# Second norms turned by transposing DMAs, gate and up weights in three pieces, and the last later-token output product inside the first feed-forward block

## Chip, core and metric

The kernel runs on one core of a Trainium2 chip. The metric is the device time of one execution in microseconds. The core has TensorE (PE, with its weight loads listed apart as PEld), VectorE (DVE), ScalarE (ACT), GpSimd (POOL) and SyncE (SP). Each runs its own list of instructions in order and waits on semaphores; DMAs are issued from SP and ACT and move data between device memory and the on-chip buffer.

## The reference

A block of a recurrent transformer over 2048 tokens of width 640, followed by a gated feed-forward layer. `x` is normed, cut into 64 segments of 32 tokens, and each segment is put behind 8 memory rows; attention runs over these 40 rows with 32 heads of 128, and the first 8 rows of the result are the memory of the next segment.

```python
for s in range(n_seg):
    xs = x[:, s * seg_len:(s + 1) * seg_len, :].copy()
    h = jnp.concatenate([mem, xs], axis=1)
    q = jnp.einsum('btd,dhe->bhte', h, Wq)
    k = jnp.einsum('btd,dhe->bhte', h, Wk)
    v = jnp.einsum('btd,dhe->bhte', h, Wv)
    scores = jnp.einsum('bhqe,bhke->bhqk', q, k) * scale
    scores = jnp.where(mask[None, None], scores, -1000000000.0)
    p = _softmax(scores, axis=-1)
    o = jnp.einsum('bhqk,bhke->bhqe', p, v)
    o = jnp.einsum('bhte,hed->btd', o, Wo)
    mem = o[:, :M, :].copy()
    outs.append(o[:, M:, :])
...
gate = jnp.einsum('bsd,df->bsf', x, W_gate)
up = jnp.einsum('bsd,df->bsf', x, W_up)
gate = gate * (gate > 0)
h = gate * up
return jnp.einsum('bsf,fd->bsd', h, W_down)
...
h = x + _A_ref(_layernorm(x, axis=-1), A_mem0, A_Wq, A_Wk, A_Wv, A_Wo, A_seg_len)
h2 = h + _B_ref(_layernorm(h, axis=-1), B_W_gate, B_W_up, B_W_down)
```

F, the width of the feed-forward layer, is 1728. Types are bf16, with sums in 32 bits.

## The kernel before

The work has three stages. First the weights Wq, Wk, Wv and Wo are loaded, and the projections of the first part of the rows that do not depend on the recurrence are made. Then the 64 segments run one after the other (`segment`, L1813). Last, the feed-forward layer runs in 4 blocks of 512 tokens (`ffn`, L1687).

A segment's own tile of 32 rows (`xT`) holds the 8 memory rows and its first 24 tokens. The last 8 tokens ("later tokens") do not depend on the recurrence before attention and are handled apart: `ln1r(r)` (L1486) norms the later tokens of 16 segments at a time (r = 0 to 3), turns them on TensorE with 20 transposes (L1496), and evicts them to `xr`; `rest` (L1538) makes their projections, which go through the staging tiles `stg` to the scratch tensors `scr_qk` and `scr_v`, and `load_rs` (L1592) brings them back for each segment. Nine of the sixteen groups of `rest` are made ahead of the segments; the others are filler between the segments' own products. The output product of the later tokens, `rest_o` (L1608, products at L1617), is made for 8 segments at a time; it is filler too, except for the last 8 segments (z = 7), whose product follows the last segment in one piece of 128 matmuls (L2018). `rest_out` (L1628) stores it into `scr_o`.

The second norm, `ln2(k)` (L1650), runs for each of the 16 tiles of 128 tokens: load x and the attention's output, add, store the sum to `scr_h`, norm, turn on TensorE with 20 transposes (`tr2`, L1669, products at L1673), evict. For k below 4 the eviction writes `xn2T`, the moving operand of the first feed-forward block; for the others it writes a tile that is stored, turned, to `scr_n` and loaded again by `ffn` (L1692). Tiles 14 and 15, which need the last segments, are called `tn2`; the others run as filler during the segments.

`ffn(b)` works on 14 chunks of the width F, 13 of 128 and one of 64 for gate and up together. For each chunk, 5 matmuls make the gate and 5 the up product (`proj`, L1695, products at L1699), ACT applies the relu, DVE multiplies (L1718). Then for 4 tiles of 128 tokens, 14 pairs of matmuls (512 and 128 columns; the second uses the weights that the first has loaded, L1732 and L1510) make the down product, DVE adds `h` in two instructions (L1739), and SP stores the tile (L1742).

The feed-forward weights lie where Wq, Wk and Wv lay. `load_f` (L2032) loads gate and up in two pieces each, 896 and 768 columns; the first waits until Wq's place is free (key `B0`), the second also for the eviction of the last segment's output (key `("osb", 1)`); Wd and the rest follow.

No order is written out by hand. `op` records each operation with the keys it reads (`r=`), writes (`w=`) and the buffers it takes (`x=`), with an estimated duration; `_Sched.schedule` then puts the operations in a fixed order on each engine, by a level that is the length of the work behind an operation plus a number from the table `BIAS` for its name and segment. `ENGINE` says which of ACT and DVE makes an eviction. The result is a static list for each engine; at run time there are only semaphore waits.

## Time and profile before

| | us |
|---|---|
| median of 3 runs | 1036.55 |
| lowest and highest | 1035.58, 1037.53 |
| the profiled execution's own time | 1038.79 |
| span of the profiled execution | 1037.1 |

The mean granted TensorE clock was 0.998. In the second part of the page, the busy tenths of the engines are given in 40 slices of the span, so that one slice is 25.9 us; slices 1 to 3 are the weight load and the early projections, slices 4 to 33 the segments, and slice 33 on the feed-forward layer:

```profile
PE   6999999999999999999999999999999989999998
DVE  5865676677767666876676577667766734232242
ACT  2236555456556664665465555645654633121210
DMA  9995111122112221311121122112221155110111
```

A digit 9 means 90% or more. The DMA engines are full while weights are loaded: in the first three slices, and to half in slices 33 and 34.

### The profile page before, as it was taken

The page shows a single profiled execution, that of the slowest core. Times are in us where ns is not written, and L with a number is a line of the kernel's source. Part 1 is how long each engine was busy: PE and PEld are TensorE (multiplying, and loading weights), DVE is VectorE, ACT ScalarE, POOL GpSimd, SP SyncE. Part 2 cuts the span into 40 slices and gives each one's busy share as a digit, 9 for nine tenths or more (in the row PEclk, how much of TensorE's full clock was granted, in tenths as well). Part 3 has the DMA queues.
Part 4 walks back from the last instruction along what each step waited for, and adds up shares of the span by engine and source line. Part 5 has one row for each costly group of instructions (what it writes and reads, how often), then busy time and mean ns, then how long its engine had stood idle before and what let it go on. Part 6 is the DMA issues. An engine that isn't in the chain of part 4 may idle for free.

```text
span 1037.1 us, 53187 instructions
## 1 busy us (share of the span) xinstructions
PE 991.5 (96%) x24820; PEld 531.0 (51%) x23828; DVE 643.2 (62%) x1400; ACT 492.0 (47%) x1165; POOL 107.7 (10%) x262
## 2 busy tenths in 40 slices
PE   6999999999999999999999999999999989999998
PEld 2345545555555555655555555555555554344443
DVE  5865676677767666876676577667766734232242
ACT  2236555456556664665465555645654633121210
POOL 2241101001000100111011001000100010000000
PEclk9999999999999999999999999999999999999999
DMA  9995111122112221311121122112221155110111
GB/s 327 405 314 128 40 38 44 34 63 65 50 27 73 55 59 33 93 46 37 50 81 54 29 66 76 44 33 74 65 52 39 59 178 175 60 58 20 32 33 44
DMA packets 119212, 84.26 MB, mean 81 GB/s; under 512 B 71556, under 2 KB 115148, under 8 KB 118988
## 3 DMA queue, kind: packets, MB, share of 16 engines
q1 hardware_dynamic: 113900, 76.56, 24.5%
q8 instruction: 191, 3.13, 1.3%
q10 hardware_dynamic: 5088, 4.30, 1.2%
q14 instruction: 33, 0.27, 0.1%
HBM read 55.05 MB, written 25.69 MB: 78 GB/s over the span
## 4 chain that ended last, share of the span: by engine, by line
PE 89%; DVE 4%; DMA 4%; issue 1%; POOL 0%; ACT 0%; SPq 0%; ACTq 0%; POOLq 0%; DVEq 0%
PE ps L1532 46%; PE ps L1699 11%; PE ps L1906 7%; PE ps L1925 7%; PE ps L1732 5%; PE ps L1617 3%; PE ps L1873 3%; PE ps L1510 2%; DMA scr_qk<-stg 2%; PE ps L1848 2%; PE ps L1834 1%; DVE xT L1646 1%; DMA big<-in_A_x_dram 1%; DVE xm L1643 1%; DMA Wq<-in_A_Wq_dram 1%
## 5 line engine op out<-in xcount | busy, mean ns | idle before, releaser
L1372 ACT ACTIVATE tok<-ps 128x512 bf16<-128x512 f32 x230 | 136.6, 597 | 158.5 <-PE ps L1532 152.5
L1532 PE MATMUL ps<-Wk,xT 128*32 128x512 bf16 x2560 | 183.3, 379 | 4.2 <-DVE xT L1646 3.1
L1532 PE MATMUL ps<-Wq,xT 128*32 128x512 bf16 x2560 | 169.7, 380 | 12.6 <-DVE xT L1646 11.8
L1532 PE MATMUL ps<-Wv,xT 128*32 128x512 bf16 x2560 | 178.3, 379 | 0.0
L1955 DVE STREAM_TRANSPOSE QT<-tok 128x512 bf16<-128x512 bf16 x128 | 90.9, 711 | 40.1 <-ACT tok L1372 37.5
L1955 DVE STREAM_TRANSPOSE KT<-tok 128x512 bf16<-128x512 bf16 x128 | 90.7, 708 | 34.2 <-ACT tok L1372 32.5
L1373 DVE CAST oT<-ps 128x320 bf16<-128x320 f32 x130 | 63.6, 491 | 76.6 <-PE ps L1878 73.5
L1532 PEld LDWEIGHTS ps<-Wq,xT 128*32 128x32 bf16 x2560 | 65.7, 97 | 85.5 <-DVE xT L1646 25.4
L1532 PEld LDWEIGHTS ps<-Wk,xT 128*32 128x32 bf16 x2560 | 63.8, 96 | 62.2 <-DVE xT L1646 9.3
L1906 PE MATMUL ps<-Wo,oT 128*32 128x320 bf16 x2048 | 92.0, 301 | 1.5 <-DVE oT L1373 1.1
L1925 PE MATMUL ps<-Wo,oT 128*32 128x160 bf16 x4096 | 86.2, 233 | 6.3 <-issue 3.8
L1716 ACT ACTIVATE g<-ps 128x512 bf16<-128x512 f32 (+1 forms) x56 | 33.4, 596 | 121.7 <-PE ps L1699 121.7
L1372 ACT ACTIVATE oT<-ps 128x320 bf16<-128x320 f32 x126 | 55.0, 437 | 67.9 <-PE ps L1878 65.4
L1925 PEld LDWEIGHTS ps<-Wo,oT 128*32 128x32 bf16 x4096 | 74.7, 97 | 21.5 <-DVE oT L1373 11.7
L1843 ACT ACTIVATE E<-ps 128x224 bf16<-128x224 f32 x128 | 45.7, 357 | 82.9 <-PE ps L1838 82.9
L1718 DVE TENSOR_TENSOR gT<-g,ps 128x512 bf16<-128x512 bf16 (+1 forms) x56 | 37.9, 686 | 68.0 <-PE ps L1699 57.3
L1532 PEld LDWEIGHTS ps<-Wv,xT 128*32 128x32 bf16 x2560 | 60.7, 96 | 36.8 <-DVE tok L1373 0.3
L1820 POOL COPY QT<-RS 128x256 bf16<-128x256 bf16 x64 | 25.6, 400 | 476.8 <-PE ps L1838 476.7
L1373 DVE CAST tok<-ps 128x512 bf16<-128x512 f32 x90 | 59.5, 662 | 22.1 <-PE ps L1532 22.0
L1372 ACT ACTIVATE ps<-seed 128x384 f32<-128x384 bf16 x110 | 50.6, 487 | 36.5 <-DVE half L1914 34.9
L1699 PE MATMUL ps<-xn2T,Wg 128*128 128x512 bf16 x260 | 63.3, 380 | 0.0
L1699 PE MATMUL ps<-xn2T,Wu 128*128 128x512 bf16 x260 | 63.2, 380 | 0.0
(95 smaller groups left out, 1451.2 us busy)
## 6 DMA issues: line engine op xcount, KB each, us to landing
RS<-scr_qk SPq DMA_DIRECT2D x63, 128.0 KB, 2.3
big<-in_A_x_dram SPq DMA_DIRECT2D x36, 160.0 KB, 3.0
Wq<-in_A_Wq_dram SPq DMA_DIRECT2D x10, 512.0 KB, 6.9
Wk<-in_A_Wk_dram SPq DMA_DIRECT2D x10, 512.0 KB, 7.8
Wv<-in_A_Wv_dram SPq DMA_DIRECT2D x10, 512.0 KB, 7.8
Wo<-in_A_Wo_dram SPq DMA_DIRECT2D x8, 640.0 KB, 11.3
scr_qk<-stg ACTq DMA_DIRECT2D x32, 128.0 KB, 6.0
scr_v<-stg SPq DMA_DIRECT2D x32, 128.0 KB, 2.9
```

The lines of the kernel that those rows point to most:

```text
L1372: return e.activation(dst, src, ACTF.Copy)
L1373: return e.tensor_copy(dst, src)
L1532: o = pe.matmul(out, lhs[c], rhs, start=(c == 0), stop=(c == DC - 1), skip_group_check=True)
L1617: o = pe.matmul(bank(bk)[p0:p0 + 32, 0:2 * SLICE], oTr[b][:, h, 32 * y:32 * y + 32], cols(h, 2 * a, 2 * a + 2), start=(h == 0), stop=(h == ...
L1699: o = pe.matmul(bank(bk)[:, 0:TB], lhs(c), xT[:, :, c * 128:(c + 1) * 128], start=(c == 0), stop=(c == DC - 1))
L1716: op("act", lambda a, t=t, lo=lo, hi=hi, bg=bg: a.activation(g1[t.at][lo:128, :], bank(bg)[0:hi, 0:TB], ACTF.Relu), r=["B2"], x=[bg, t], d ...
L1718: op("dve", lambda v, t=t, lo=lo, j=j, bu=bu: v.tensor_tensor(gT[lo:128, j, :], g1[t.at][lo:128, :], bank(bu)[lo:128, 0:TB], ALU.mult), r= ...
L1732: pe.matmul(bank(ba)[:, 0:512], lhs, Wd[:, j, 0:512], start=(j == 0), stop=(j == FC - 1), skip_group_check=True)
L1843: op("act", lambda a: a.activation(E[:, g, :, 0:56], sco(BS[g]), ACTF.Exp, scale=SCALE), r=["table"], w=[("E", g)], x=[BS[g]], dur=0.36, n ...
L1906: o = pe.matmul(bank(BA)[p0:p0 + 32, 0:2 * SLICE], oT[:, 4 * jj + i, XR:40], cols(h, 2 * b2, 2 * b2 + 2), start=(i == 0 and jj < 2), stop= ...
L1925: o = pe.matmul(bank(BW)[32 * j:32 * j + 32, 0:SLICE], oT[:, 16 + 4 * jj + i, XR:40], cols(h, j, j + 1), start=(i == 0 and jj == 0), stop= ...
L1955: op("dve", lambda v, tb=tb, dst=dst: v.transpose(dst, tok[tb.at][:, :].rearrange("p (h r) -> p h r", r=32)), w=[("QT" if p == 0 else "KT" ...
```

## The change

Five things are edited, and the tables `BIAS` and `ENGINE` are replaced by others, so that the order of operations differs everywhere.

1. Turns by DMA. `ln2` has no TensorE transposes and no eviction after them. For k below 4, SP issues a transposing DMA from the normed tile to `xn2T`. For the others the normed tile is stored as it is, and `ffn` loads it with a transposing DMA. `ln1r` does the same for r = 2 and 3; r = 0 and 1 stay on TensorE.
2. Gate and up weights come in three pieces, of 384, 640 and 640 columns. The first waits for `B0`, the others also for the last segment's output eviction. The loads of the normed tiles of block 1 (and 3) wait for that eviction as well.
3. The last later-token output product (z = 7) stands in the first feed-forward block: it waits for the up products of chunks 0 to 2 (keys `guz`), and chunk 3's gate product waits for it (key `roz`).
4. The norms 14 and 15 are recorded after the first block's chunks.
5. The last token tile's down product is made in two passes, 14 matmuls of 512 columns and then 14 of 128 with their own weight loads; each half is added and stored by itself.

The estimate of one POOL copy rises from 0.8 to 1.08 in the early stage; that alters the planner's order only.

```diff
+FPIECES = ((0, 384), (384, 1024), (1024, 1664))
...
+        slot = r == 1 and EARLY > 4
+        if r > 1:
+            op("sp", lambda e: e.dma_start_transpose(xr[slot][:, :, :], big[xt.at][:, :]), x=[xt], w=[("xr", slot)],
+               dur=0.5, lat=3.5, chan=("tp", 2), name="ln1rT", xfer=0.5)
+            return
...
-        bt = B("tr")
-
-        def tr2(pe):
-            o = None
-            for c in range(DC):
-                for a in range(4):
-                    o = pe.matmul(bank_bf(bt)[32 * a:32 * a + 32, c * 128:(c + 1) * 128],
-                                  big[at.at][:, c * 128 + 32 * a:c * 128 + 32 * a + 32], ident[:, :], is_transpose=True)
-            return o
-
-        op("pe", tr2, r=["ident"], x=[at, bt], dur=0.28, n=40, name=nm + "T")
         if k < 4:
-            either(lambda e, en: copy(e, en, xn2T[0][:, u, :], bank_bf(bt)[:, 0:640]),
-                   r=["late"], w=[("xn2T", 0, u)], x=[bt], dur=ev(640, True), name=nm + "Tev")
+            op("sp", lambda e: e.dma_start_transpose(xn2T[0][:, u, :].rearrange("p (c t) -> p c t", c=DC), big[at.at][:, :]),
+               r=["late"], w=[("xn2T", 0, u)], x=[at], dur=0.5, lat=3.5, chan=("tp", 2), name=nm + "T", xfer=0.5)
             return
-        either(lambda e, en: copy(e, en, big[x2.at][:, :], bank_bf(bt)[:, 0:640]), x=[bt, x2], dur=ev(640, True),
-               name=nm + "Tev")
-        op("sp", lambda e: e.dma_start(scr_n[k], big[x2.at][:, :]), w=[("scr_n", k)], x=[x2], dur=0.4, lat=2.2,
+        op("sp", lambda e: e.dma_start(scr_n[k], big[at.at][:, :]), w=[("scr_n", k)], x=[at], dur=0.4, lat=2.2,
            chan=("n", 2), name=nm + "nd")
...
         for u in range(4 if b else 0):
-            op("sp", lambda e, u=u: e.dma_start(xT[:, u, :], scr_n[4 * b + u]), r=[("scr_n", 4 * b + u)] + (["B1"] if home else []),
-               w=[("xn2T", home, u)], dur=0.4, lat=2.4, chan=("xn", 4), name="xnld")
+            op("sp", lambda e, u=u: e.dma_start_transpose(xT[:, u, :].rearrange("p (c t) -> p c t", c=DC), scr_n[4 * b + u]),
+               r=[("scr_n", 4 * b + u)] + (["B1", ("osb", 1)] if home else []), w=[("xn2T", home, u)], dur=0.5, lat=3.5, chan=("tp", 2), name="xnld")
...
         for j in range(FC):
             t = _Slot("g1", range(3))
+            if b == 0 and j == 3:
+                z = NSEG // 8 - 1
+                rest_o(z, B("rest"), (0, 8), [("guz", n) for n in range(3)], "roz")
+                rest_out(z)
             if j < FC - 1:
                 bg, bu = banks(0, 1, 2, 3), banks(0, 1, 2, 3)
-                proj(bg, lambda c, j=j: Wg[:, c, j * 128:j * 128 + 128], ("Wg", 2 * j // FC), (), [bu])
-                proj(bu, lambda c, j=j: Wu[:, c, j * 128:j * 128 + 128], ("Wu", 2 * j // FC))
+                n = [f0 <= 128 * j < f1 for f0, f1 in FPIECES].index(True)
+                proj(bg, lambda c, j=j: Wg[:, c, j * 128:j * 128 + 128], ("Wg", n), ["roz"] * (b == 0 and j == 3), [bu])
+                proj(bu, lambda c, j=j: Wu[:, c, j * 128:j * 128 + 128], ("Wu", n), (), (), [("guz", j)] * (b == 0 and j < 3))
...
+        if b == 0:
+            for k in range(NQ - 2, NQ):
+                ln2(k)
...
+            last = b == NBLK - 1 and u == 3
+            if last:
+                for bk, c0, c1 in ((ba, 0, 512), (bb, 512, 640)):
+                    def f(pe, bk=bk, c0=c0, c1=c1, u=u):
+                        o = None
+                        for j in range(FC):
+                            o = pe.matmul(bank(bk)[:, 0:c1 - c0], gT[:, j, u * 128:(u + 1) * 128], Wd[:, j, c0:c1],
+                                          start=(j == 0), stop=(j == FC - 1), skip_group_check=True)
+                        return o
+                    op("pe", f, r=[("gT", j) for j in range(FC)] + ["Wd0", "Wd1"], x=[bk], dur=3.02 if c0 == 0 else 0.82, n=28,
+                       mode="f", name="down")
+            for j0 in (0, FC // 2) if not last else ():
...
+                if last:
+                    op("sp", lambda e, hb=hb, k=k, c0=c0, c1=c1: e.dma_start(out_ap[k * 128:(k + 1) * 128, c0:c1], tl[hb.at][:, c0:c1]),
+                       r=[("hl", k, c0)], w=[("out", k, c0)], beside=[hb], dur=0.42, lat=2.2, chan=("out", 4), name="outdma")
...
-        if s == NSEG - 1:
-            rest_o(s // 8, B("rest"), (0, 8))
-            rest_out(s // 8)
...
-    for hf, (f0, f1) in enumerate(((0, FH), (FH, FL))):
+    for n, (f0, f1) in enumerate(FPIECES):
         for wt, src, nm in ((Wg, B_W_gate, "Wg"), (Wu, B_W_up, "Wu")):
-            load_f(wt[:, :, f0:f1], src[:, f0:f1].rearrange("(c p) f -> p c f", p=128), (nm, hf), ["B0"] + [("osb", 1)] * hf, D * (f1 - f0) * 2)
+            load_f(wt[:, :, f0:f1], src[:, f0:f1].rearrange("(c p) f -> p c f", p=128), (nm, n), ["B0"] + [("osb", 1)] * (n > 0), D * (f1 - f0) * 2)
...
-    for k in normed + list(range(NQ - 2, NQ)):
+    for k in normed:
         ln2(k)
```

31 lines of the change are left out of this document (15 added, 16 removed), and 1402 rows, old and new, of tables (BIAS, ENGINE).

## The prediction

> **What bounds the kernel now.** I read the page first, for the busy shares and the chain that ended last.
>
> ```profile
> span 1037.1 us, 53187 instructions
> PE 991.5 (96%) x24820; PEld 531.0 (51%) x23828; DVE 643.2 (62%) x1400; ACT 492.0 (47%) x1165; POOL 107.7 (10%) x262
> PE 89%; DVE 4%; DMA 4%; issue 1%; POOL 0%; ACT 0%; SPq 0%; ACTq 0%; POOLq 0%; DVEq 0%
> ```
>
> TensorE is busy for 96% of the span and carries 89% of the chain. The share hides three stages with different limits: loading and early projections until about 89 us, 64 recurrent segments until about 849 us, feed-forward until the end. So the next view is the busy time in single stretches: one stretch per segment, then the changeover.
>
> ```profile
> 232.34:244.20 11.86, 11.82 (x372) 6.87 (x352) 9.01 (x21) 7.30 (x19) 0.99 (x3) 1.00 0.36 99
> 507.99:521.31 13.32, 12.22 (x364) 6.64 (x348) 9.98 (x24) 7.19 (x18) 0.99 (x3) 1.00 0.26 73
> 605.80:618.73 12.93, 12.22 (x364) 6.62 (x348) 9.74 (x22) 7.49 (x19) 0.99 (x3) 1.00 0.27 73
> 642.74:654.41 11.67, 11.49 (x355) 6.17 (x330) 8.06 (x18) 6.89 (x17) 2.08 (x4) 1.00 0.17 50
> 702.55:715.34 12.79, 12.23 (x364) 6.64 (x348) 9.58 (x22) 7.63 (x19) 0.99 (x3) 1.00 0.27 76
> 715.34:727.26 11.92, 11.92 (x372) 6.91 (x352) 9.02 (x21) 7.15 (x19) 0.99 (x3) 1.00 0.35 97
> 823.01:834.94 11.93, 10.45 (x320) 5.84 (x308) 7.26 (x17) 6.20 (x15) 0.99 (x3) 1.00 0.04 9
> ```
>
> The columns are the stretch, its length, then busy time and instruction count of PE, PEld, DVE, ACT and POOL, clock, DMA share and GB/s. The last row is a segment with its own 320 products and nothing else; TensorE idles 11.93 - 10.45 = 1.48 us in it, and still it takes 11.93 us. The fourth row carries 35 more products and takes 11.67 us. A segment is thus bound by its chain through the engines; filler work is free until it fills the idle time, and taking filler away gains only where a segment stands above some 11.7 us. Rows two, three and five are such segments, 13.32, 12.93 and 12.79 us, crowded with filler.
>
> In the feed-forward stage TensorE never waits. Between the two stages it does:
>
> ```profile
> 846.00:848.40 2.40, 0.02 (x1) 0.00 (x0) 0.00 (x0) 0.00 (x0) 0.00 (x0) 1.00 0.97 334
> 849.10:852.50 3.40, 3.40 (x60) 3.40 (x53) 0.28 (x1) 0.00 (x0) 0.00 (x0) 0.50 0.56 151
> 852.50:855.00 2.50, 2.50 (x76) 2.23 (x68) 0.00 (x0) 0.00 (x0) 0.00 (x0) 1.00 1.02 336
> 844.96 1.06 PE ps L1925 x49
> 846.02 2.41 issue
> 848.42 0.46 PE ps L1925 x15
> 849.02 6.02 PE ps L1617 x128
> 855.04 22.77 PE ps L1699 x105
> ```
>
> The first three rows are stretches, the other five the chain in order of time. In the middle of 64 equal products of the last segment (49 before, 15 after) TensorE stops for 2.41 us. No semaphore stands between them; the chain calls it issue. All engines are idle meanwhile, and the DMA engines are 97% busy. Then the granted clock is 0.50 for 3.4 us, which falls on the last later-token output product (L1617).
>
> **The change part by part.**
>
> *Weight pieces.* What keeps the DMA engines busy in that stretch is this, from SP's timeline and the list of DMA issues:
>
> ```profile
> 838.78 0.39 SPq L2036 DMA_DIRECT2D Wg<-in_B_W_gate_dram  x1
> 839.21 0.53 SPq L2036 DMA_DIRECT2D Wu<-in_B_W_up_dram  x1
> 839.99 2.03 SPq L1692 DMA_DIRECT2D xn2T<-scr_n  x4
> 849.41 0.38 SPq L2036 DMA_DIRECT2D Wg<-in_B_W_gate_dram  x1
> Wg<-in_B_W_gate_dram SPq DMA_DIRECT2D x1, 1120.0 KB, 5.6
> Wu<-in_B_W_up_dram SPq DMA_DIRECT2D x1, 1120.0 KB, 9.3
> xn2T<-scr_n SPq DMA_DIRECT2D x12, 160.0 KB, 2.6
> q8 instruction: 191, 3.13, 1.3%
> ```
>
> 2240 KB of weights and 4 x 160 KB of norms are 2880 KB; at the 334 GB/s of the stall's stretch that is 8.8 us, from 839.2 to about 848, where the stall ends. Queue 8 brings instructions (its columns are packets, MB and share): 3.13 MB in 191 packets is 16.4 KB a packet, and there is one packet for every (24820 + 23828) / 191 = 255 TensorE instructions. My reading is that one such packet stood behind the burst and TensorE ran dry. In the new kernel the first pieces are 384 instead of 896 columns, 480 KB each, and the four norm loads also wait for the last segment's output (osb 1). 960 KB at 334 GB/s are 2.9 us, done by about 842, four microseconds before TensorE needed the packet. So the stall goes: -2.41 us.
>
> The Trainium skill speaks against this reading: "Runtime: NRT & Kernel Launch", Instruction fetch mechanics, says that crossing a 16 KiB block costs one tail-bump, mostly hidden, since the sequencer dispatches more slowly than blocks are filled. For 190 of the 191 packets the trace agrees: no other stop of this length is put to issue. By that rule the 2.41 us would have another cause and stay, which is the first rival below.
>
> *Clock.* The product of L1617 took 6.02 us on the chain, 3.4 us of it at half clock: 1.70 us lost. The second way to price it is by an equal shape at full clock:
>
> ```profile
> 831.04 1.27 PE L1906 MATMUL ps<-Wo,oT 128*32 128x320 bf16 x32 [0.23 <-DVE oT L1373]
> 843.33 0.73 PE L1906 MATMUL ps<-Wo,oT 128*32 128x320 bf16 x16 [0.59 <-DVE oT L1373]
> ```
>
> Sixteen more cost 0.54 us, so 128 cost 0.73 + 7 x 0.54 = 4.51 us, 1.5 us under 6.02. I take -1.6 us, since without the stall nothing else there idles for long.
>
> *Moving the product* itself takes nothing off TensorE: its 4.5 us now lie after three chunks of gate and up. Those take 3 x 2.16 = 6.5 us (one pair is 10 matmuls, and 105 matmuls took 22.77 us). What the order buys is cover: pieces two and three go out at the last output eviction, about 2.4 us earlier than the 849.41 above, and 6.5 + 4.5 = 11.0 us pass before chunk 3 needs piece two, 1600 KB or 4.8 us at 334 GB/s. Without that cover TensorE would wait some 2 us there. The norms 14 and 15, behind this product, feed only block 3, tens of microseconds later; their output stores, loads and h store stay on SP as before.
>
> *Transposes off TensorE.* The sixteen groups of the second norms and two of the four first ones go. Their rows, with one group inside the feed-forward stage:
>
> ```profile
> L1673 PE MATMUL ps<-ident,big 128*32 128x128 bf16 x320 | 7.7, 220 | 0.8 <-issue 0.8
> L1372 ACT ACTIVATE big<-ps 128x640 bf16<-128x640 bf16 x10 | 7.0, 704 | 4.1 <-PE ps L1673 4.1
> 876.57 1.24 PE L1699 MATMUL ps<-xn2T,Wu 128*128 128x512 bf16 x5
> 877.74 0.46 PE L1673 MATMUL ps<-ident,big 128*32 128x128 bf16 x20
> 878.14 0.39 PE L1732 MATMUL ps<-Wd,gT 128*128 128x512 bf16 x1
> ```
>
> 7.7 / 16 = 0.48 us a group. The two groups in the feed-forward stage lie on the bound: -0.96 us. Fourteen of the second norms and one first norm (r = 3) lie in segments. There each gains between 0 (idle segment) and 0.48 us: together 0 to -7.2 us. The rows 232.34 and 715.34 above hold such a group and have no idle time left, at 11.86 and 11.92 us; the floor is 11.67, so such a segment gives 0.19 to 0.25 us. About half of the fifteen are this full, the others less. I take 0.17 on the mean, -2.5 us. Their evictions (0.70 us on ACT) leave engines that are no bound: nothing, except what is in this mean.
>
> *Transposes on SP.* No transposing DMA is in this trace. Below, the plain norm load above lands in 2.6 us; above, the slowest issue of the burst, 2080 KB of Wd, takes 13.8 us. I take the near end, since a transposing load carries the same 160 KB. Twelve are in the feed-forward stage: block 2's and 3's go out a whole block ahead ((1033.6 - 855)/4 = 45 us); block 1's are behind the weights (3200 + 2080 + 240 KB from about 847 on, 16.5 us at 334 GB/s, so until 864), and its first chunk is needed between 880 and 898 (four down products of 14 x 0.27 us, priced below, can go ahead). Even two in flight at 13.8 us each, 27.6 us, come to 892. So nothing on the path. Four more are for norms 0 to 3 in the segments, hundreds of microseconds early. SP waits there for the norm itself instead of for its eviction, so what is queued behind (segment loads) waits no longer than now.
>
> The tight one is r = 2, early:
>
> ```profile
> 67.93 0.66 DVE L1458 TENSOR_SCALAR big<-big,mv,rstd 128x640 bf16<-128x640 bf16 x1
> 72.64 0.58 SPq L1579 DMA_DIRECT2D scr_v<-stg  x1
> 74.77 0.70 ACT L1372 ACTIVATE xr<-ps 128x640 bf16<-128x640 bf16 x1 [8.44 <-DVE stg L1373]
> 79.86 1.26 PE L1532 MATMUL ps<-Wq,xr 128*32 128x512 bf16 x20
> ```
>
> Normed by 68.6, written by ACT at 75.5, used at 79.86. SP's next issue stands at 72.64, but SP must now hold this DMA until the last product of rows 0 to 3 has read the old contents; behind it stand the value stores and the second segment's loads. At 2.6 us it lands before 79.9 even if issued at 75; at 13.8 us it is 9 us late, and TensorE waits in order. I take 0, with +9 as the far end and -0.5 (its TensorE group) as the near one.
>
> *The end.* The last token tile's product is done in two passes, 512 then 128 columns.
>
> ```profile
> 1032.82 0.38 PE L1732 MATMUL ps<-Wd,gT 128*128 128x512 bf16 x1
> 1033.09 0.38 PE L1732 MATMUL ps<-Wd,gT 128*128 128x512 bf16 x1
> L1739 DVE TENSOR_TENSOR tl<-tl,ps 128x512 bf16<-128x512 bf16 x16 | 11.0, 688 | 56.2 <-PE ps L1510 56.2
> ```
>
> A pair takes 0.27 us, 0.216 of it the wide half, so 14 narrow ones take 14 x 0.056 = 0.78 us if their weight loads hide. If each load of 98 ns is serial it is 2.2 us (+1.4). I take 0.78: the 0.69 us addition then lies under it: -0.7 us.
>
> *New order.* Every bias and engine choice of the planner differs, so fillers fall into other segments. The 63 segments from 89.25 to 846.9 us average 12.03 us against the 11.67 us floor: 22 us is the most a better order can give, and as much again a bound for a worse one. With no row for which way, I take 0.
>
> Sum: -2.41 - 1.6 - 0.96 - 2.5 - 0.7 = -8.2 us. From the profiled span of 1037.1 us that is 1028.9. The median of the three runs is 1036.55, 0.5 us below that span (the profiled run's own time is 1038.79, with 1.7 us around the span), so the same sum gives 1028.4 us: -0.8%.
>
> **Rivals.** *The stall stays or moves.* Pieces two and three still make 3200 KB in flight, and the moved product's 256 instructions run through a whole packet amid it. For: a stall needs only one packet behind a burst. Against: 6.5 us of slow instruction use precede it. Then 2.41 + 1.6 are not gained: 1032.4 us.
>
> *Crowded segments, slower.* Fillers are pushed together in the recurrence: the 13.32 us row is 1.4 us above the bare segment of 11.93. From six more such segments on, the 8.2 us are used up; ten would give +14 - 8.2, about 1042 us. For: all the order is new, and three such segments stand in it now. Against: fewer fillers remain to be placed.
>
> *A late early transpose.* r = 2 lands as late as Wd, +9: about 1037 us, no change.
>
> *A better order.* The three crowded segments go to the floor, 1.65 + 1.26 + 1.12 = 4.0 us, and the segments freed of transposes gain twice my mean, 2.5 us more: 1028.4 - 6.5 = 1022 us.
>
> **Numbers.** Forecast 0.52; stall stays 0.20; crowded 0.12; late transpose 0.06; better order 0.10. This kernel's measurement tells 0.2%, 2.1 us, from no change. Faster are the first, second and last cases: 0.82. The late transpose is mostly no change, with the edge of the crowded case: 0.06. Slower is the rest: 0.12. The range runs from 1021 to 1036 us.
>
> **What would show it.** The issue wait of 2.4 us is gone and the clock row stands at 1.00 through the changeover; the L1617 product at about 4.5 us amid the gate and up products with no wait around it; no waits of TensorE on xn2T or xr; segments with a mean of about 12.0; one short addition after the last matmul. It is wrong if segments above 12.7 us multiply, or TensorE waits for a transposing DMA.

## The result, and the profile after

| | median us | lowest to highest | runs |
|---|---|---|---|
| before | 1037.74 | 1034.89 to 1041.35 | 20 |
| after | 1040.51 | 1036.79 to 1043.51 | 20 |

The ratio is 1.0028, with a 95% interval of 1.0016 to 1.0039: the change makes the kernel slower by about 2.8 us, where 8 us less were forecast. The profiled execution of the change is its fastest of the 20 (1036.79 us, span 1035.0). So its span is 2.1 us *below* the span before, while the median is above, and no span alone can be read as the result here.

The first view is busy time by stage. A stage ends where VectorE turns the memory rows of segment 1, and of segment 63, so the middle one holds 62 segments. Columns as in the prediction: stretch, length, then busy time of PE, PEld, DVE, ACT and POOL, clock, DMA share, GB/s. Before:

```profile
0.00:89.25 89.25, 75.53 (x1448) 33.44 (x1436) 57.56 (x113) 27.52 (x59) 28.44 (x56) 1.00 0.91 322
89.25:834.94 745.69, 720.43 (x21904) 411.67 (x21152) 521.49 (x1175) 422.76 (x1030) 77.48 (x203) 1.00 0.20 54
834.94:1037.10 202.16, 195.56 (x1476) 85.92 (x1240) 64.20 (x114) 41.69 (x77) 1.78 (x4) 0.99 0.24 77
```

After, with the two longest segments below the stages:

```profile
0.00:90.42 90.42, 74.06 (x1424) 33.17 (x1416) 56.43 (x111) 27.44 (x60) 28.83 (x56) 1.00 0.91 319
90.42:837.17 746.75, 717.08 (x21608) 410.23 (x20856) 511.97 (x1156) 423.34 (x1033) 77.58 (x202) 1.00 0.21 55
837.17:1035.00 197.83, 192.29 (x1424) 83.80 (x1214) 64.46 (x113) 40.81 (x76) 1.78 (x4) 1.00 0.29 78
...
498.43:511.50 13.07, 12.16 (x376) 7.06 (x356) 7.25 (x16) 6.74 (x16) 0.99 (x3) 1.00 0.15 33
523.64:537.07 13.43, 12.28 (x356) 8.00 (x336) 9.45 (x23) 7.01 (x19) 0.99 (x3) 1.00 0.36 102
```

Read the middle rows first. TensorE has 720.43 - 717.08 = 3.35 us less to do in the segments, the relief that the prediction counted on, and yet they are 1.06 us longer: its idle time there went from 25.3 to 29.7 us. The last stretch is 4.3 us shorter. TensorE's timeline of the change (start, us, operation, in brackets the idle time before it and what ended it) shows three places of that stretch and the end:

```profile
847.19 1.29 PE L1937 MATMUL ps<-Wo,oT 128*32 128x160 bf16 x64
...
855.13 4.53 PE L1618 MATMUL ps<-Wo,oTr 128*32 128x320 bf16 x128
...
887.56 0.39 PE L1739 MATMUL ps<-Wd,gT 128*128 128x512 bf16 x1 [1.33 <-DVE gT L1711]
...
1031.37 0.94 PE L1729 MATMUL ps<-Wd,gT 128*128 128x128 bf16 x14
```

The 64 products run through without a stop, the moved product takes 4.53 us (4.5 forecast) with no wait around it, and the narrow last pass 0.94 us (0.78 forecast). These came as predicted. The 1.33 us before 887.56 did not. The chain of waits gives the work that leads there (start, us, what):

```profile
880.27 3.02 DMA big<-in_A_x_dram
883.31 0.49 DVE big L1662
883.80 0.81 DVE stat L1442 x2
...
886.95 0.56 DVE gT L1711
887.56 0.39 PE ps L1739
```

VectorE works in order. It holds the gated products of the last chunks (gT) behind the sums of the norms 14 and 15, whose loads SP issued only at 880. The list of DMA issues and the packet count tell what a turning DMA is. The twelve of the feed-forward land in 2.9 us at the median, a plain norm load of before in 2.6. The packets under 512 B are 83636; a kernel below (plain18), with the same list and plain DMAs in the place of the 18 turns, has 71828, so a turn of 160 KB brings 656 of them, about 250 B each.

```profile
xn2T<-scr_n SPq DMA_TRANSPOSE x12, 2.9
DMA packets 131032, 85.19 MB, mean 82 GB/s; under 512 B 83636, under 2 KB 126972, under 8 KB 130812
```

### The profile page after: what moved, and what is told of

Read it like the earlier page. It is cut to its first block, busy times and chain, and to the rows that moved or that the text cites. A ratio compares the mean times of both kernels' runs of the same rounds, so it can differ in the third digit from the quotient of the medians.

```text
span 1035.0 us, 52462 instructions
## 1 busy us (share of the span) xinstructions
PE 983.4 (95%) x24448; PEld 527.2 (51%) x23482; DVE 632.9 (61%) x1379; ACT 491.6 (47%) x1168; POOL 108.2 (10%) x262
## 2 busy tenths in 40 slices
DMA packets 131032, 85.19 MB, mean 82 GB/s; under 512 B 83636, under 2 KB 126972, under 8 KB 130812
## 5 line engine op out<-in xcount | busy, mean ns | idle before, releaser
L1368 ACT ACTIVATE tok<-ps 128x512 bf16<-128x512 f32 x241 | 143.2, 596 | 160.1 <-PE ps L1533 141.6
L1918 PE MATMUL ps<-Wo,oT 128*32 128x320 bf16 x2048 | 91.4, 300 | 1.5 <-DVE oT L1369 1.3
L1832 POOL COPY QT<-RS 128x256 bf16<-128x256 bf16 x64 | 25.6, 401 | 480.8 <-PE ps L1850 480.6
L1368 ACT ACTIVATE ps<-seed 128x384 f32<-128x384 bf16 x117 | 53.6, 487 | 39.0 <-DVE half L1926 38.8
L1369 DVE CAST tok<-ps 128x512 bf16<-128x512 f32 x79 | 52.0, 658 | 17.2 <-PE ps L1533 17.2
```

The lines of the kernel that those rows point to most:

```text
L1368: return e.activation(dst, src, ACTF.Copy)
L1369: return e.tensor_copy(dst, src)
L1832: op("pool", lambda e: e.tensor_copy(QT[:, :, 0:XR], RS[rb][:, 0:256].rearrange("p (h k) -> p h k", k=XR)), r=[("RSqk", rb)], w=["QTx"], d ...
L1918: o = pe.matmul(bank(BA)[p0:p0 + 32, 0:2 * SLICE], oT[:, 4 * jj + i, XR:40], cols(h, 2 * b2, 2 * b2 + 2), start=(i == 0 and jj < 2), stop= ...
```

## The experiments

Four theories were at hand when the experiments were planned. T: the transposing DMAs themselves are the loss. S, the mechanism of T: they hold SP, whose plain issues take 0.3 to 0.6 us. L, another one: the turned data land late. O: the loss is in the order that the planner emits from the new tables. "Change" below is the kernel after. Before was timed again beside each group of kernels, and each ratio is to those runs.

### The change again, its parts, and the old tables

Four kernels: the change unaltered; the kernel before with the pieces, the held norm loads and the moved product; before with all turning DMAs, the hold of the norm loads that belongs to them, and nothing else; the whole change with the tables of before.

```diff
 changeover_only:    +FPIECES, +("osb", 1) for the norm loads, rest_o(z = 7) inside ffn(0); BIAS, ENGINE of before
 turn_only:          -tr, tr2 (PE) and their evictions   +dma_start_transpose (SP); BIAS, ENGINE of before
 change_old_tables:  the change; BIAS, ENGINE of before
```

> The changed kernel as it stands, for a second profile, since its first profiled execution (1036.79 us) was the fastest of its 20 while their median is 1040.51. Theory O (the new order of the early stage and the segments costs what the changeover gains): the stretch from the last segment's first product to the end stays about 198 us (202 before), and the segments and the early stage are 4 to 8 us longer than the 847 us of before. Theory M (in most executions the changeover stalls, the first profile being a lucky one): the segments stay within 2 us of before's, and the last stretch is 201 us or more. Time 1040 to 1041 us by both.

> The kernel before with its own tables, and of the change only the three weight pieces with the norm loads behind the last eviction, the moved last output product, and the norms 14 and 15 behind the first block's chunks. The order of every engine up to the last segment is that of before. Theory O: -2.5 to -4 us against before (stall and half clock gone, a possible new wait of 1.3 us on the multiplications inside the feed-forward stage), ratio 0.996 to 0.998. Theory M: not faster, or slower, ratio 1.000 to 1.003. Theory T (the transposing DMAs cost): as theory O.

> The kernel before with its own tables, and of the change only the turns by transposing DMAs (second norms and the first norms 2 and 3). Theory T (SP holds the transposing DMAs, or they disturb the other transfers): +4 to +7 us against before, and waits on xr, xn2T or on loads queued behind them. Theory O: -2 to +1 us, since the order is nearly that of before and 0.48 us a group leaves TensorE.

> The whole change of the operations, with the tables (biases and engine choices) of the kernel before. Theory O (the new tables' order is the loss): -4 to -7 us against before, ratio 0.993 to 0.996. Theory T: the loss stays, ratio 1.000 to 1.004.

| | median us (runs) | ratio to before | interval |
|---|---|---|---|
| again | 1040.36 (12) | 1.0030 | 1.0013 to 1.0048 |
| changeover_only | 1038.18 (12) | 0.9996 | 0.9982 to 1.0009 |
| turn_only | 1048.27 (6) | 1.0102 | 1.0076 to 1.0127 |
| change_old_tables | 1046.34 (6) | 1.0076 | 1.0051 to 1.0101 |

The loss repeats. In the second profile of the change TensorE does not stop at the changeover either, and its last stretch is 198.38 us, so theory M of the first expectation, that the first profile was a lucky one, is out. The changeover alone neither gains nor loses what can be told, where -2.5 to -4 us or no gain at all had been expected: the stop and the half clock are gone from its profile, but TensorE waits 1.7 us in three places inside the first feed-forward block (0.75 us for the relu's output the longest), and its last stretch is 200.4 us where before's is 201.3 on the mean of five profiles. The third and fourth rows lie above what any theory had forecast. I first read the third row as the price of the turns, 10 us, and the fourth against O. The trace of turn_only seemed to give the mechanism. SP's timeline in segment 21:

```profile
341.55 1.42 SPq L1673 DMA_TRANSPOSE xn2T<-big  x1
343.01 0.58 SPq L1664 DMA_DIRECT2D big<-scr_o  x1
343.63 0.42 SPq L1662 DMA_DIRECT2D big<-in_A_x_dram  x1
```

and VectorE's:

```profile
346.00 0.49 DVE L1666 TENSOR_TENSOR big<-big,big 128x640 bf16<-128x640 bf16 x1 [1.40 <-DMA big<-in_A_x_dram]
...
346.93 0.49 DVE L1906 TENSOR_TENSOR half<-ps,half 128x320 bf16<-128x320 f32 x1
```

The turn holds SP for 1.42 us, the two loads behind it come later, VectorE waits 1.40 us for them, and the work behind it (`half`) is what the recurrence needs. That is S as it looks in a trace. The next four kernels tested it.

### Spare turns, turns from another engine, six turns back

Spare turns: before, and for the norms 0 to 2 one DMA more whose result nobody reads, in an order that differs from before's in a few places. Spare copies: the same with plain DMAs, identical in order.

```diff
+        if k < 3:
+            op("sp", lambda e: e.dma_start_transpose(xn2T[0][:, 3, :]..., big[at.at][:, :]),   # spare_copies: dma_start
+               beside=[at], r=["late"], w=[("xn2T", 0, 3)], dur=0.5, lat=3.5, chan=("tp", 2), name="dummy")
 turns_from_act:     turn_only with op("act", ...) for the turns of norms 0 to 3
 change_tensor_six:  the change with r = 2, 3 and norms 0 to 3 turned on TensorE
```

> The kernel before, with everything turned on TensorE as before, and three transposing DMAs more: those of the second norms 0 to 2, on SP at the place where the change has them, into a part of the feed-forward tile that the fourth norm overwrites later; nobody reads them. Theory S (what the change loses is SP's time: a transposing DMA holds SP's queue for 1.2 to 1.4 us where a plain one takes 0.33 to 0.45, the loads of the next second norm stand behind it, and VectorE, which works in order, holds the recurrence's copies back while its addition waits for them): the segments with such a DMA get longer as in the kernel with the turns alone (there 14 by 1.8 us, 21 and 22 by 2.5 and 2.1), so 2 to 6 us in all, 1.002 to 1.006. Theory L (the loss is that the turned norm lands 2.7 to 4 us after its issue, later than TensorE gave it): nobody waits for these, so 0.999 to 1.001.

> The same as the kernel with three spare turns, in the same order on every engine, but the three spare DMAs are plain copies of the same 160 KB. Theory S: SP is held 0.3 to 0.5 us by each, so at most 1 us, 0.999 to 1.001, and the segments 14, 21 and 22 are within 0.6 us of before. If it is the bytes that disturb (traffic of the DMA engines), it costs as much as the spare turns.

> The kernel with the turns alone (1.0102 of before), with the four turns of the norms 0 to 3 issued by ScalarE in place of SP. Theory S: the segments 14, 21 and 22 lose their 1.8 to 2.5 us, less what 1.3 us on ScalarE cost there: 1.004 to 1.008. Theory L: it stays at 1.009 to 1.012.

> The whole change with its tables, but the six norms that are turned out of SBUF (the token rows of r = 2 and 3, the second norms 0 to 3) go back to TensorE and PSUM; the twelve turns of stored norms in the feed-forward stay DMAs. If the six are what the change loses: the early stage gets 2 to 3 us back and the segments 1 to 2 us, 0.996 to 0.999 of before against 1.003 for the change. If it is the new order or the twelve: it stays at 1.001 to 1.005.

| | median us (runs) | ratio | interval | segments us | TensorE idle in them |
|---|---|---|---|---|---|
| spare_turns | 1040.28 (10) | 1.0013 | 0.9997 to 1.0029 | 745.66 | 25.6 |
| spare_copies | 1038.97 (10) | 1.0003 | 0.9989 to 1.0017 | 746.63 | |
| turn_only (above) | | 1.0102 | | 754.77 | 39.7 |
| turns_from_act | 1050.76 (4) | 1.0101 | 1.0074 to 1.0129 | 762.13 | |
| change_tensor_six | 1050.75 (6) | 1.0117 | 1.0098 to 1.0137 | 759.68 | 34.6 |

In before's order S fell for the segments: three turns more on SP make them no longer (745.66 against 745.69 us), though they held SP for 2.3, 1.5 and 1.3 us. At the third, the two loads stand behind the turn on SP just as in turn_only (at 343.14 and 343.94 us), and segment 21 takes 11.97 us there, not 14.24. Segment 14 was 1.4 us longer, and with plain copies 1.0; others made up for it.

And taking six turns *out* of the change costs as much as putting eighteen into the kernel before. There it is the order: segment 1 takes 22.82 us, where the change's takes 11.75, because the planner turns r = 2 so late (at 89.8 us) that its products, most of which the change makes ahead of the segments, fall into it. The likely common cause is the table: with operations for which it was not searched, either table gives an order that is 8 to 12 us worse. In the traces, turn_only's lists on SP and VectorE differ from before's in dozens of places. For turn_only this is not shown, though. Of its 9.1 us in the segments 8.3 lie in segments 14, 21, 22 and 52, the first three with a turn in them or just ahead, and no kernel has its order with the turns made plain; L, whose number turns_from_act met, has no test of its own in that order either. So these four kernels mix order and turns and give no price of a turn, and the first reading does not follow from them. From here on the order is held fixed.

### One order, other contents

Plain18: the change, every engine's list as it is, but the DMAs do not turn; plain6 the six from SBUF alone. Before_less_twelve: before's lists, with 1 of 20 TensorE pieces of a turn and, in the place of its eviction of 640 columns, a copy of 32 left for norms 4 to 15. Order_kept: changeover_only and the narrow end, those remainders holding the order, and twelve turning loads.

```diff
 change_plain18, change_plain6
-   e.dma_start_transpose(dst, src)
+   e.dma_start(dst, src)
 before_less_twelve, order_kept (norms 4 to 15)
-   op("pe", tr2, ...)
+   op("pe", lambda pe: pe.matmul(bank_bf(bt)[0:32, 0:128], big[at.at][:, 0:32], ident[:, :], is_transpose=True), ...)
```

> The whole change, instruction for instruction in its own order on every engine, but the eighteen transposing DMAs are plain copies of the same 160 KB (the norms reach the products unturned: the turning is left out). Theory T (the transposing DMAs themselves are what the change loses: SP's issue of 1.2 to 2.9 us against 0.33 to 0.5, landing 2.6 to 4.8 us): 2 to 4 us less than the change, 0.999 to 1.001 of before. Theory O (the order that the planner emits for the changed work is what loses, whatever the form of these DMAs): within 1 us of the change, 1.002 to 1.004.

> The same, but only the six DMAs that turn out of SBUF (token rows of r = 2 and 3, second norms 0 to 3) are plain copies; the twelve in the feed-forward turn. If theory T holds and the six before the changeover carry the price: as with all eighteen, 0.999 to 1.001. If it is the twelve: 1.002 to 1.004, while the kernel with eighteen plain ones is at 0.999 to 1.001. Theory O: both at 1.002 to 1.004.

> The kernel before, in its own order on every engine, but of the TensorE turns of the second norms 4 to 15 only one of twenty pieces is done, and of their copies out of PSUM 32 of 640 columns (their turning is left out). It prices alone what the prediction counted as TensorE's gain: ten groups in the segments (0.17 us each, 1.7 us) and two in the feed-forward part (0.96 us). If TensorE's time sets the segments: 0.997 to 0.9985. If the recurrence or the memory rows set them: 0.9990 to 1.0005, with only the two of the feed-forward part to see in the last stretch.

> The order of before up to the last segment, with the pieces and the moved product as in the kernel with the changeover alone (0.9996), the narrow last pass of the change, and the twelve stored norms turned by DMA in the feed-forward; in the place of their TensorE groups one piece of twenty, and of their copies 32 columns, keep the order; the other six are turned on TensorE as before. Theory O: nothing of the segments is lost, so the sum is 0.5 us of the changeover, 0.7 us of the end, 1 to 2.7 us of the turns: 0.996 to 0.9985. Theory T with the price in the twelve: 1.000 to 1.003.

| | median us (12 runs) | ratio | interval | segments us | idle in them | last stretch us |
|---|---|---|---|---|---|---|
| change_plain18 | 1036.60 | 0.9991 | 0.9978 to 1.0005 | 747.16 | 29.4 | 196.3 |
| change_plain6 | 1039.93 | 1.0012 | 0.9998 to 1.0027 | 748.08 | 30.2 | 198.3 |
| before_less_twelve | 1038.95 | 1.0012 | 0.9995 to 1.0028 | 743.06 | 26.0 | 202.3 |
| order_kept | 1041.19 | 1.0022 | 1.0005 to 1.0039 | 743.13 | 25.4 | 203.0 |

Two things follow. First, in the change's own order the eighteen turns cost (1.0029 - 0.9991) x 1038 = 3.9 us by the times (some 2 to 6 with the intervals), and by the profiles nothing in the segments and 1.5 to 2.1 us in the last stretch. Plain6, at 1.0012, fell between its two forecasts: that would be 2.2 us for the twelve turns and 1.7 for the six, neither clear of the scatter. In the last stretch the stall on gT is there in the change, in its second profile and in plain6 (1.3, 1.8, 1.6 us) and gone in plain18. SP and VectorE show why. SP of the change, from the third and fourth turn on:

```profile
867.53 4.37 SPq L1680 DMA_TRANSPOSE xn2T<-scr_n  x2
871.94 0.56 SPq L2005 DMA_DIRECT2D scr_o<-osb  x1
...
878.85 0.91 SPq L1660 DMA_DIRECT2D big<-scr_o  x2
879.80 0.91 SPq L1658 DMA_DIRECT2D big<-in_A_x_dram  x2
```

VectorE of the change:

```profile
882.86 0.94 DVE L1662 TENSOR_TENSOR big<-big,big 128x640 bf16<-128x640 bf16 x2 [4.03 <-DMA big<-in_A_x_dram]
```

SP and VectorE with plain copies:

```profile
869.73 0.54 SPq L2005 DMA_DIRECT2D scr_o<-osb  x1
...
876.78 0.91 SPq L1660 DMA_DIRECT2D big<-scr_o  x2
877.73 0.91 SPq L1658 DMA_DIRECT2D big<-in_A_x_dram  x2
```

```profile
880.90 0.91 DVE L1662 TENSOR_TENSOR big<-big,big 128x640 bf16<-128x640 bf16 x2 [1.99 <-DMA big<-in_A_x_dram]
```

The store of the last segment's output (osb) leaves SP at 871.94 instead of 869.73, each entry behind it is 2.1 us later, and VectorE waits 4.03 instead of 1.99 us. Here S holds. In order_kept the same lateness stops TensorE for 2.7 us at the remainder of norm 14's turn; it had been expected at 0.996 to 0.9985.

Second, in before's order the segments get shorter when TensorE has less to turn: 743.06 and 743.13 us here and 742.47 in order_exact below, against 745.69 and 746.20 in before's two profiles and 744.2 to 746.6 in four others with all turns on TensorE. On the means, 742.9 and 745.6, that is 2.7 us. In the change's order they are 746.75 to 748.5 us in six profiles, whether its DMAs turn or not, with as little TensorE work: 717.08 us above. The 3.6 us or more between the two are the new tables': the order and the choice of engines. The time of before_less_twelve does not follow its segments: it had 0.997 to 0.9985 to reach by them and came to 1.0012, between 0.9995 and 1.0028. Its last stretch has the stop of before (2.67 us) and half clock after it; what else makes the difference stays open.

### The turns behind the loads, and where the rest is

Later_turns: the change, with the second block's four turning loads held until the load for norm 15 has landed. Change_plain_rows: the change with r = 2 and 3 as plain copies. Order_kept_later and order_exact: order_kept with the later turns; in the first the two remainders of norms 14 and 15 go too, and the order slips from segment 52 on; the second keeps it exactly. Changeover_and_end: changeover_only and the narrow last pass, all norms on TensorE. And before once more.

```diff
 later_turns, order_kept_later, order_exact
     op("sp", lambda e: e.dma_start(big[at.at][:, :], scr_o[...]), beside=[at],
+       w=[("lo", k)], ...)                                              # ln2(k)
-       r=[("scr_n", 4 * b + u)] + (["B1", ("osb", 1)] if home else []), ...)
+       r=[("scr_n", 4 * b + u)] + (["B1", ("osb", 1)] if home else []) + [("lo", NQ - 1)] * (b == 1), ...)   # ffn(b)
 change_plain_rows
-   e.dma_start_transpose(xr[slot][:, :, :], big[xt.at][:, :])
+   e.dma_start(xr[slot][:, :, :], big[xt.at][:, :]...)
```

> The whole change with one dependency more: the four turning loads of the second feed-forward block are issued on SP behind the loads of the last two second norms (14 and 15), in place of between the weight loads ahead of them. With plain DMAs the last stretch of the change took 196.3 us, with turning ones 197.8 to 198.4, and the stall of 1.3 to 1.8 us at the last gated product went. Theory S (SP's time ahead of those loads): the stall goes here too, the last stretch is 196 to 197 us, 1.3 to 2 us less than the change: 1.0008 to 1.0018. Rival (the turned data are late wherever they stand): a wait of the second block's first product for the norms, 1 us or more, appears in its place, and the time stays at 1.002 to 1.004.

> The change in its own order, with only the two turns of token rows (r = 2, which lies ahead of the segments, and r = 3) as plain copies. If these two carry what the six cost together (1.0028 to 1.0012 of before, 1.7 us): 1.0008 to 1.0018. If it is the second norms 0 to 3, or nothing but scatter: 1.002 to 1.0035.

> The kernel that keeps the order of before, with the twelve turns by DMA, now with the second block's turns behind the loads of the last two norms and no TensorE piece for these two. From the rows: segments 743 us as in the two kernels with fewer TensorE turns in the order of before (745.7 before), last stretch 196 to 198 in place of 202, so 5 us less than before: 0.994 to 0.998. If its profile shows these lengths and the time does not follow, the early stage takes it back.

> The kernel before, for a second profile. How far do the stages vary by themselves? Early stage 88 to 94 us, segments 744 to 747, last stretch 200 to 202.5: the stall at the changeover is there only in some executions.

> As the kernel with the kept order and the later turns (0.9981), but with the order of before kept exactly up to the last product of the segments; there the order had slipped from segment 52 on, and segment 54 took 14.06 us in place of 12.0. Theory O: segments 743 to 744 us, last stretch 196.4 to 198.5, 0.994 to 0.9975. If the segments are as before and it is no faster than the kernel it comes from: 0.9975 to 0.999.

> The kernel before with the pieces, the moved product and the narrow last pass alone; every norm is turned on TensorE as before, in the order of before. It says what the twelve turning DMAs are worth once they stand in the right place: 0.9996 of the changeover alone less 0.7 us of the end is 0.9989; 0.9975 to 1.000.

| | median us (runs) | ratio | interval | early us | segments us | last stretch us |
|---|---|---|---|---|---|---|
| later_turns | 1039.10 (12) | 1.0004 | 0.9991 to 1.0016 | 92.06 | 748.04 | 196.3 |
| change_plain_rows | 1039.63 (12) | 0.9999 | 0.9982 to 1.0015 | 92.04 | 748.50 | 198.0 |
| order_kept_later | 1036.94 (12) | 0.9981 | 0.9967 to 0.9995 | 94.15 | 746.39 | 196.4 |
| before_again | 1038.90 (8) | 0.9995 | 0.9979 to 1.0011 | 90.93 | 746.20 | 199.8 |
| order_exact | 1037.00 (12) | 0.9991 | 0.9977 to 1.0005 | 90.55 | 742.47 | 199.6 |
| changeover_and_end | 1036.41 (12) | 0.9991 | 0.9976 to 1.0005 | 90.93 | 745.36 | 199.6 |

Later_turns decides S for the feed-forward. One dependency more gives 2.5 us (1.0028 to 1.0004; some 1 to 4 with the intervals, and a little more than S had forecast), no wait appears in the stall's place, and the last stretch is that of plain18. SP and VectorE of later_turns:

```profile
872.29 0.91 SPq L1658 DMA_DIRECT2D big<-in_A_x_dram  x2
874.22 2.59 SPq L1680 DMA_TRANSPOSE xn2T<-scr_n  x2
```

```profile
877.37 0.89 DVE L1662 TENSOR_TENSOR big<-big,big 128x640 bf16<-128x640 bf16 x2
```

The sums of the norms start 5.5 us earlier than in the change, though the segments before them ended 2.9 us later, and wait for nothing. Before_again shows the stop at the changeover too, 1.73 us long, but no half clock after it; the product that follows takes its full-clock time:

```profile
849.94 0.46 PE L1925 MATMUL ps<-Wo,oT 128*32 128x160 bf16 x15 [1.73 <-issue]
...
850.31 4.58 PE L1617 MATMUL ps<-Wo,oTr 128*32 128x320 bf16 x128
```

Order_kept_later is the only kernel whose interval lies below 1: 2 us faster than before, and just outside its forecast. Its interval overlaps those of order_exact and changeover_and_end, so it is not shown to beat these. It has its own mishaps: one segment of 14.06 us where the order slipped, and TensorE idle for 17.3 us in the early stage where before's two profiles have 13.7 and 14.3. Order_exact put the order right. Its segments are the shortest of all, 742.47 us, but its last stretch has 2.3 us of waits that the change does not have, 1.3 us for weights (Wg) and 1.0 us for gT. Its profiled execution of 1034.34 us is its fastest, and its median does not follow: the forecast of 0.994 to 0.9975 was missed. It cannot be told from changeover_and_end, which met its forecast (0.9989); a gain of the twelve turns over TensorE is not shown by times.

Change_plain_rows is a miss of another kind: its time says that the two row turns cost 3 us, its profile shows no stage shorter. The gT stall is still there, TensorE waits for no turned xr in either kernel, and the early stage, 92.04 us, lies between the change's two, 90.42 and 92.78. What r = 2 costs stays open.

## Why the prediction was wrong, point by point

**Stall at the changeover, -2.41.** Right in kind. Kernels with before's changeover stop there in all five profiles, for 2.41, 1.73, 2.59, 1.89 and 2.67 us. Turn_only and turns_from_act have the two pieces of before but hold the norm loads back; they stop for 1.03 us. With three pieces and held loads there is no such stop, in the change or in any other kernel but one. That one is change_tensor_six, which stops for 0.88 us after its burst is over, with the DMA engines idle (its timeline, and the stretch of the stop):

```profile
862.41 0.45 PE L1924 MATMUL ps<-Wo,oT 128*32 128x320 bf16 x6 [0.88 <-issue]
...
861.50:862.40 0.90, 0.02 (x2) 0.00 (x0) 0.08 (x1) 0.02 (x1) 0.30 (x1) 1.00 0.00 0
```

So the stops of 1.7 to 2.7 us go with the large burst, and a short one can come without any traffic. That an instruction packet stands behind the burst was argued and not shown. The first rival, that the stall stays, is out for the change. The Trainium skill ("Runtime: NRT & Kernel Launch", Instruction fetch mechanics) calls the crossing of a block mostly hidden; no run here shows whether it is what stops TensorE.

**Half clock, -1.6.** Right for the profiled execution, where the product took 6.25 us against 4.53 at full clock; that this execution had it was luck, for three profiles of five have it. It followed the stops of 2.41, 2.59 and 2.67 us, not those of 1.73 and 1.89. The five last stretches are 202.2, 199.8, 202.2, 199.9 and 202.3 us, 201.3 on the mean, so 0.9 us of this term and the one above was not there to gain on average.

**Feed-forward groups and end, -0.96 and -0.7.** Right in their sum. The four terms up to here give 202.2 - 5.7 = 196.5 us for the last stretch; without the new stall it is 196.3. The end by itself is 0.8 us, changeover_and_end against changeover_only (199.6 and 200.4). The two groups by themselves are not shown: before_less_twelve, which leaves 1 of 20 pieces of them, has a last stretch of 202.3 us, 2.67 us of it the stop and about 2 the half clock, and without these it is only some 0.4 us shorter than before's.

**"So nothing on the path."** The step that failed first. For the twelve turns I worked out when their data are needed, and these were in time. I did not ask what stands behind them on SP. With four turns amid the weight loads SP is 2.2 us late after them; behind them are the last stores, then the loads of norms 14 and 15, then VectorE's sums, then gT, then TensorE. The prediction's own sentence on these norms, that they "feed only block 3, tens of microseconds later", is true of their result and false of their place in VectorE's list. It cost 1.3 to 1.8 us by the profiles, where nothing had been counted, and 2.5 by the times.

**"SP waits there for the norm itself", in the segments.** Held in the change's order, where plain18's segments (747.16 us) lie between those of the change's two profiles (746.75 and 747.34), and for three spare turns in before's.

**Segments, -2.5, and "New order ... I take 0".** The second failure. The relief of TensorE was priced too low, if anything: with before's order the segments show 2.7 us for ten turns (two of the twelve lie behind the segments), 0.27 us each where the prediction took 0.17 for each of fifteen. But the new order idles TensorE for 29.7 instead of 25.3 us in the segments and takes back all of it and 1.1 to 1.7 us more. The prediction had the range for this, 22 us both ways, and a rival on this side, crowded segments at 1042 us, with a chance of 0.12; its place is right, its picture (ten crowded segments) only in part. Three stand above 13 us, 16, 35 and 37: 13.03, 13.07 and 13.43 us, where order_exact has 12.72, 11.89 and 12.33. That is 2.6 of the 4.3 us by which the change's segments are longer than order_exact's. They come again in the change's second profile (13.02, 12.88 and 13.69 us), while before's second profile has no segment above 12.7; of the three that the prediction took for crowded, 36, 44 and 52, only 36 comes again in other profiles of that order, and not in all. Where the rest is lost stays open. TensorE's longest group of waits in the segments does not say it (what ended it, us in total, times, longest; before, then after, then order_exact):

```profile
PE ps L1532 <- DVE xT L1646: 14.4, 29, 0.6
```

```profile
PE ps L1533 <- DVE xT L1647: 18.7, 40, 0.6
```

```profile
PE ps L1533 <- DVE xT L1647: 17.8, 37, 0.7
```

It is larger in both kernels that give TensorE less to do, and order_exact, with nearly as much of it, has the shortest segments of all.

In the early stage the new order trades. Ahead of 60 us TensorE idles less (1.7 us against 3.3 between 16 and 60 us), behind 60 us more; there TensorE's waits begin with these, before, then after:

```profile
PE ps L1532 <- DVE stg L1373: 1.2, 2, 1.0
PE ps L1532 <- ACT tok L1372: 0.2, 1, 0.2
```

```profile
PE ps L1533 <- ACT stg L1368: 2.3, 2, 1.9
PE ps L1937 <- DVE oT L1369: 0.9, 1, 0.9
```

The first of the latter is in all six profiles of that order, 1.8 to 2.1 us long: ScalarE's list has a store's issue that waits for GpSimd, and the copy that frees TensorE's bank stands behind it.

**The sum.** Between 1028.4 and 1040.5 lie 12.1 us. The three runs of before were low by 1.2 us against twenty. The stop and the half clock were oversized by 0.9 on the mean. The segments gave +1.1 for -2.5, 3.6 us. The eighteen turns cost 3.9 us by the times, of which 1.3 to 1.8 is the gT stall. That is 9.6 us; 2.5 us stay open, and so does where the turns' 3.9 us lie beyond the stall. The stages of the change's second profile, an execution of 1040.24 us and so at the median, give the other way to add up. Its span of 1038.5 us is 9.6 above the forecast span of 1028.9: 3.5 in the early stage, 4.2 in the segments and 1.9 behind them. What is left, 2.5 us, is 0.3 to the median and 2.2 of base: the sum came from an execution of 1038.79 us and was taken off a median of 1036.55. The 3.5 us of the early stage are not shown to be the change's: in ten profiles of before's order it takes from 89.25 to 94.15 us, 91.4 on the mean, in six of the change's from 89.56 to 92.78, 91.2 on the mean. The prediction had started from the shortest of them.

## What to carry to other kernels

When an instruction moves to a queue, price the time for which it holds the queue, and follow what stands behind it through every in-order engine to the one that bounds; that its own result is in time proves little. A planner's table belongs to the set of operations that it was searched for: alter the set, and a change of 8 to 12 us may say more of the table than of the operation, so test contents in a frozen order. Where executions of one list scatter by more than the gain that is asked for, a profile shows which wait has gone, and only the times show what it was worth.

## What the runs showed of the hardware

- A transposing DMA of 160 KB holds SP for longer than a plain one. The twelve of the feed-forward in the change, then the plain loads in the same places of the same list in plain18 (ns at the least, at the median and at the most):

```profile
L1680 SPq DMA_TRANSPOSE xn2T<-scr_n x12: 1199/1273/2934, 850.6 to 932.5; - x12
DMA to landing us min/median/max: 2.7/2.9/9.3
```

```profile
L1680 SPq DMA_DIRECT2D xn2T<-scr_n x12: 319/432/2741, 850.6 to 929.6; - x12
DMA to landing us min/median/max: 2.2/2.5/9.2
```

  The longest of either kind stand amid the weight loads. From issue to landing a turn takes 0.4 us more at the median; the four of the norms 0 to 3 land in 4.0 us against 3.1. The Trainium skill ("Advanced Engine Details and Errata", X-Bar Transpose (TRN2)) says that these DMAs are as fast as regular ones; the trace comes near that for the landing and not for the issue.
- Half clock came after stops of TensorE of about 2 us, not after each of them. In the early stage of two kernels with the change's order, plain18 first, then change_plain_rows:

```profile
62.70:64.70 2.00, 0.00 (x2) 0.01 (x2) 0.00 (x0) 0.60 (x1) 1.94 (x2) 1.00 1.07 379
64.70:68.10 3.40, 3.40 (x36) 1.44 (x40) 1.88 (x3) 0.00 (x0) 3.21 (x4) 0.53 1.07 375
```

```profile
64.60:66.67 2.07, 0.00 (x1) 0.01 (x2) 0.00 (x0) 0.60 (x1) 2.01 (x2) 1.00 1.07 380
66.67:70.00 3.33, 3.33 (x64) 1.67 (x68) 1.89 (x3) 0.00 (x0) 3.15 (x4) 1.00 1.08 365
```

A stop of 2.0 us drew it, one of 2.1 us did not, and with the clock at 0.53 only 36 products ran in 3.40 us.
